# The order of loads at two places: the last quad's packs and two rows of a column product

## The chip, the cores and the metric

The kernel runs on one core of a Trainium2 chip. The metric is device time in microseconds for one execution, as the median of several runs. A core has five engines with instruction queues of their own: TensorE (PE: matmuls, with weight loads shown as PEld), VectorE (DVE), ScalarE (ACT), GpSimd (POOL) and SyncE (SP). In this kernel SyncE issues all the transfers between the memory off the core and the on-chip memory. Each engine works through its queue in the order in which it was written; semaphores order the engines among each other.

## What is computed

Four layers are applied to x of 2048 rows by 640 columns in float32. Layers 0 and 2 are attention with a sliding window, layers 1 and 3 mix x with Fourier matrices:

```python
def attention(x, wqkv, wo):            # H = 32 heads of 20, window W = 256
    q, k, v = heads(x @ wqkv)
    scores = q @ k.T * 20 ** -0.5      # for 0 <= i - j < 256, else -1e9
    return softmax(scores) @ v, heads joined, @ wo

def fourier(x):
    a, b = x @ hid_re.T, x @ hid_im.T
    return seq_re @ a - seq_im @ b

x = x + attention(layernorm(x)); x = x + fourier(layernorm(x))
x = x + attention(layernorm(x)); x = x + fourier(layernorm(x))
```

## The kernel before

Products are made with three matmuls on a high and a low part of each operand (`split`, L226 to L235: ScalarE writes the high part, VectorE or GpSimd the low part).

**An attention layer.** The 32 heads form eight quads of four heads. `heads` (L608) runs one loop of 16 steps per quad, 128 steps in all, plus a lead of ten. A step makes three things at different depths: the raw scores of row block s = step + 10 (`s_head`, L633), whose row maxima VectorE takes at L638; the transposed scores of step t = step (`t_pair`, L661, exponentials at L671, masks on GpSimd at L677 and L681); and the product with v for v = step - 1 (`pv`, L696). Every four steps the maxima are transposed, and two small transfers write them into the query tile (`m_rows`, L651).

Into each step `fill` puts a share of other matmuls (L259, in `lockstep`). First come the last projections of q and k (`project`), counted in units: 600 in all. The share is the largest of several quotients, among them "all units by step 96" (`ROWS_AT`) and "the units that the next pack needs, by the step at which it is due". Once the projection is done, `prepare(4)` (L949) posts the loads of the first four rows of x for the output parts (`load_y`, L954, tile "big", called y0, y1 and so on here), and the fill goes on with the output parts (`partials`, L956), nine matmul pairs a step. The result of a part is added to its row of x by VectorE at L980. Loads of head outputs and their factors (L861, L867) are requested along the way.

A projected piece goes to memory off the core (`qk_d`, L526) and comes back "packed" in the layout that the scores want. A pack (`pack`, L584) covers one quad and a quarter of the rows (512): twelve transfers of 80 KB at L596, the first six into the key tile and the other six into the query tile. They are deferred in triples: three at the step at which the pack is due and three at each of the next three steps. There are two key and two query tiles, for even and odd quads. The list `due` holds when each pack is due, counted in s; the last quad's four packs have entries of their own, in `LAST_DUE`. Its first raw scores are made at s = 112, that is step 102, and the second quarter's at step 106.

**A Fourier layer.** `fourier` (L1595) ends with a product by columns, in eight groups of two row blocks. Groups 1 to 5 of layer 1 (where `more` is true), and groups 1 to 7 of layer 3, take `seven` (L1711): seven products instead of eight, in the order b11, t1, b21, t2, t3, b22, t4. The right half of the odd row (`x22`) is added to after t1, the left half of the even row (`x11`) after b21. Between these additions (L1664) VectorE makes the low parts of later operands (`cut_part`, L1592), so what holds up an addition holds up the cuts behind it. Rows of x come in through `load_x` (L1649) into a ring of five tiles that other loads share, and go out through `store_x` (L1661). A row is requested by `load_x` at the head of a group's loop (L1814) or by `rows_after`, which `seven` calls behind b21. In layer 1 `rows_after` requests only one row from group 4 on, because weight chunks for the next attention layer use the ring as well.

Of the kernel before, what the change touches and what calls it, by code (L numbers as in the profile page):

```python
# [21 lines left out]
NQ = H // 4  # L22
# [8 lines left out]
AHEAD = 8  # L31
# [1 line left out]
AHEAD_X = 4  # L33
AFTER = 4
ROWS_AT = 96
LAST_DUE = (-10, -7, 2, 6)
FIRST = 7
LATE = 9
BACK = 2
# [26 lines left out]
class Net:  # L66
# [541 lines left out]
    def heads(self, xsrc, xdst, hook):  # L608
# [98 lines left out]
        def finish(quad, bk):  # L707
# [10 lines left out]
            def store():  # L718
# [6 lines left out]
        total = NCH * NSB * per_piece  # L725
        done = [2 * NSB * per_piece]

        due = [(16 * q + (4 * j - AHEAD if q < NQ - 1 else LAST_DUE[j]),
                ((-(-160 * (q + 1) // P) - 1) * NSB + 2 * (j // 2) + 2) * per_piece, q, j)
               for q in range(1, NQ) for j in range(NSB)]  # L730
        self.xsrc = xsrc
# [47 lines left out]
        for step in range(-LEAD, steps + 1):  # L779
# [11 lines left out]
            if due and s >= due[0][0]:  # L791
                while done[0] < due[0][1]:
                    fill(15)
                q, j = due.pop(0)[2:]
# [800 lines left out]
    def fourier(self, xsrc, xdst, more):  # L1595
# [53 lines left out]
        def load_x(*ts):  # L1649
            for t in ts:  # L1650
                if t < NB and t not in raws:
                    raws[t] = self.raw()
                    nc.sync.dma_start(raws[t], xsrc[t * P:(t + 1) * P, :])

        def rows_after(g):
            load_x(2 * g + 2)
            if not more or g < 4:
                load_x(2 * g + 3)

        def store_x(t):  # L1660
            nc.sync.dma_start(xdst[t * P:(t + 1) * P, :], raws.pop(t))  # L1661
# [24 lines left out]
        def eight(g, z):  # L1686
            t = 2 * g + z
            for n in range(2):
                if z:
                    coming(g + 1, n)  # L1690
                elif g:
                    self.cut_part(self.quarter(g, n, 1))
            if z == 0:
                if g:
                    self.load_u(g + 1, 1)
                    self.load_u(g + 2, 0)
                if more and g == 6:
                    before(11)
            before(t)
            ops = [self.made.popleft() for _ in range(2)]  # L1700
            for hf in range(2):
                p = self.bank("y", 320)
                cs = slice(hf * 320, (hf + 1) * 320)
                self.all3(p, [((ops[k // KC][0][k % KC], ops[k // KC][1][k % KC]),
                               (wc[k][0][:, cs], wc[k][1][:, cs])) for k in range(2 * KC)])
                add(nc.vector, raws[t][:, cs], p, raws[t][:, cs])
                if z and hf:
                    differences(g + 1)
            store_x(t)

        def seven(g, halfway):  # L1711
# [29 lines left out]
            self.cut_part(a21)  # L1741
            self.load_u(g + 1, 1)
            rows_after(g)
            halfway()
            product(y, "t2")
# [19 lines left out]
        def before(t):  # L1765
            if not more:
                return
            if t == 8:
                self.tmp = cuts(self.take_qk("kp", 0, F32), D)
                self.home = [self.home[i] for i in (2, 3, 0, 1)]  # L1770
            if 8 <= t < 11:
                for k in range(2):
                    self.prep_load(xdst, 2 * (t - 8) + k)
                if t < 10:
                    self.load_chunk(t - 8)
            i = t - 12
            if 11 <= t < NB - 1:
                for k in range(2):
                    self.prep_stats(2 * i + 2 + k)
                for k in range(2):  # L1780
                    self.prep_norm(2 * i + 2 + k)
            if t == NB - 1:
                self.prep_stats(8)
                self.prep_norm(8)

        def behind(t):
            if more and t >= 12:
                i = t - 12
                if i < 2:
                    self.cut_chunk(i)  # L1790
                for k in range(2):
                    self.prep_turn(2 * i + k)
                if i < 3:
                    for k in range(2):
                        self.prep_load(xdst, 6 + 2 * i + k)
# [15 lines left out]
        self.leave()  # L1811
        self.u_sum = [self.slot_tile(n, 512, F32)[:, :320] for n in ("rr1", "rr2", "vq2")]
        for g in range(NB // 2):
            load_x(2 * g + 1)  # L1814
            if g in sevens:
                before(2 * g)
                seven(g, lambda: before(2 * g + 1) if g < 5 else None)
            else:
                rows_after(g)
                for z in range(2):  # L1820
                    eight(g, z)
                    behind(2 * g + z)
# [73 lines left out]
```

## Time and profile before

| | |
|---|---|
| median of 3 runs | 2179.72 us (2177.11 to 2182.58) |
| the profiled execution | 2178.74 us, its span 2177.0 us |
| mean granted TensorE clock | 0.997 |
| TensorE busy | 2105.7 us, 97% |
| VectorE busy | 1625.7 us, 75% |
| ScalarE busy | 1138.3 us, 52% |
| GpSimd busy | 919.7 us, 42% |
| transfers | 414.78 MB, mean 191 GB/s |

In a row of a timeline stand the start and the duration in us, the engine (SPq is the issue of a transfer by SyncE), the line, the operation, the tiles (written <- read), the shapes and a count xN of neighbours merged into the row. In brackets stands how long the engine stood idle before it and what ended that. A row of the waits names the waiting engine and line, what it waited for, the total in us, how often, and the longest. A row of the stretches has the stretch, its length, the busy time of PE, PEld, DVE, ACT and POOL with the number of instructions, the granted clock, the busy share of the transfer engines and GB/s.

Layer 0's steps 90 to 104 lie at about 403 to 455 us, the same steps of layer 2 about 1086 us later; groups 4 and 5 of layer 1's column product lie at about 1037 to 1068 us.

### The profile page before, as it was taken

What the parts mean: (1) busy time and instruction counts of PE and PEld (TensorE: products, weight loads), DVE (VectorE), ACT (ScalarE), POOL (GpSimd) and SP (SyncE); (2) the same over time, 40 slices, a digit from 0 to 9 for tenths busy, and PEclk for the clock granted to TensorE, in tenths of its full rate; (3) what the DMA queues carried; (4) which work ended last, traced back from release to release, by engine and by line L of the source; (5) the groups of instructions that cost most, each with busy time, mean ns of one, the idle gap of its engine ahead of it and who ended that gap; (6) DMA issues with size and microseconds to landing.
All of it is one profiled execution on the core that took longest, in us unless ns stands there. A gap on an engine that the chain in (4) does not pass through costs nothing.

```text
span 2177.0 us, 48902 instructions
## 1 busy us (share of the span) xinstructions
PE 2105.7 (97%) x17812; PEld 1774.9 (82%) x17812; DVE 1625.7 (75%) x3973; ACT 1138.3 (52%) x2131; POOL 919.7 (42%) x1538
## 2 busy tenths in 40 slices
PE   7999999899999999999999999998899999999999
PEld 7987777677868888889999877776778888888899
DVE  6358888776898879786761588887868968687776
ACT  3117777656554545552341277776566645455432
POOL 3037777765513232321230377767655032331222
PEclk9999999999999999999999999999999999999999
DMA  5556666675656564757645566667855454546653
GB/s 184 176 162 191 197 189 200 204 232 165 206 188 216 177 228 160 256 186 271 209 156 172 161 191 198 189 203 202 233 157 185 141 180 135 173 135 229 240 205 136
DMA packets 234288, 414.78 MB, mean 191 GB/s; under 512 B 40768, under 2 KB 87360, under 8 KB 234048
## 3 DMA queue, kind: packets, MB, share of 16 engines
q1 hardware_dynamic: 234048, 411.66, 58.8%
q8 instruction: 141, 2.31, 0.4%
q14 instruction: 99, 0.81, 0.1%
HBM read 283.77 MB, written 126.62 MB: 189 GB/s over the span
## 4 chain that ended last, share of the span: by engine, by line
PE 81%; DVE 8%; DMA 4%; ACT 3%; issue 3%; POOL 1%; SPq 0%; ACTq 0%; DVEq 0%; POOLq 0%
PE banks L1419 29%; PE banks L259 13%; PE banks L241 13%; PE banks L1729 8%; PE banks L696 7%; PE banks L661 6%; PE banks L633 5%; DVE banks L638 1%; DVE qp L234 1%; ACT pt L671 1%; PE banks L343 1%; DMA kp<-qk_d 1%; PE banks L646 1%; DMA x_d<-x 0%; DVE big L980 0%
## 5 line engine op out<-in xcount | busy, mean ns | idle before, releaser
L638 DVE CUSTOM_DVE_ANT_0 banks<-banks,mask 128x384 f32<-128x384 f32 (+2 forms) x1024 | 527.0, 556 | 112.1 <-PE banks L633 94.7
L671 ACT ACTIVATE pt<-banks 128x768 f32<-128x768 f32 (+2 forms) x512 | 393.6, 771 | 176.4 <-PE banks L661 82.7
L677 POOL TENSOR_SCALAR_AFFINE_SELECT pt<-pt 128x256 f32<-128x256 f32 x512 | 219.0, 428 | 217.4 <-ACT pt L671 197.8
L259 PE MATMUL banks<-big,wc 64*128 64x512 f32 x1920 | 272.5, 394 | 0.4 <-DVE pt L444 0.4
L661 PE MATMUL banks<-qp,kp 61*128 61x384 f32 (+2 forms) x1024 | 209.5, 380 | 32.3 <-DVE mc L638 26.8
L696 PE MATMUL banks<-pt,vq 128*32 128x128 f32 x5760 | 210.4, 277 | 3.5 <-ACT pt L671 3.5
L633 PE MATMUL banks<-kp,qp 60*128 60x384 f32 (+2 forms) x1024 | 209.6, 351 | 1.9 <-DVE mc L638 1.8
L259 PEld LDWEIGHTS banks<-big,wc 64*128 64x128 f32 x1920 | 187.9, 185 | 21.3 <-DVE pt L444 0.5
L228 ACT ACTIVATE qp<-pt 128x512 fp32r<-128x512 f32 (+1 forms) x200 | 123.1, 625 | 135.0 <-DVE pt L1350 54.0
L681 POOL TENSOR_SCALAR_AFFINE_SELECT pt<-pt 128x256 f32<-128x256 f32 x448 | 187.6, 419 | 0.0
L661 PEld LDWEIGHTS banks<-qp,kp 61*128 61x128 f32 x1024 | 108.0, 184 | 95.6 <-DVE mc L638 73.1
L234 DVE TENSOR_TENSOR qp<-pt,qp 128x512 fp32r<-128x512 f32 (+1 forms) x198 | 155.9, 796 | 38.2 <-ACT qp L228 36.4
L696 PEld LDWEIGHTS banks<-pt,vq 128*32 128x32 f32 x5760 | 141.6, 109 | 51.6 <-issue 35.7
L1419 PE MATMUL banks<-qp,big 128*128 128x512 f32 x648 | 153.5, 390 | 0.0
L228 ACT ACTIVATE c<-pt 128x512 fp32r<-128x512 f32 x146 | 90.7, 625 | 115.8 <-POOL pt L1328 56.7
L633 PEld LDWEIGHTS banks<-kp,qp 60*128 60x128 f32 x1024 | 126.3, 186 | 25.9 <-DVE mc L638 17.0
L1348 POOL TENSOR_TENSOR pt<-pt,pt 128x512 f32<-128x512 f32 x32 | 46.8, 1461 | 237.8 <-DMA pt<-c 125.9
L638 DVE DVE_READ_ACCUMULATOR2_ANT mc<- 128x1 f32 x1024 | 143.9, 141 | 0.0
L1419 PEld LDWEIGHTS banks<-qp,big 128*128 128x128 f32 x648 | 120.7, 188 | 25.0 <-POOL qp L234 0.9
L234 DVE TENSOR_TENSOR c<-pt,c 128x512 fp32r<-128x512 f32 x144 | 116.6, 812 | 27.1 <-ACT c L228 24.3
L1419 PE MATMUL banks<-qp,xc 128*128 128x512 f32 x480 | 117.6, 391 | 3.8 <-DVE xc L234 2.3
L1419 PEld LDWEIGHTS banks<-qp,xc 128*128 128x128 f32 x480 | 89.5, 188 | 25.4 <-DVE xc L234 5.3
(241 smaller groups left out, 4401.1 us busy)
## 6 DMA issues: line engine op xcount, KB each, us to landing
pt<-c SPq DMA_DIRECT2D x166, 512.0 KB
qk_d<-c SPq DMA_DIRECT2D x80, 512.0 KB
kp<-qk_d SPq DMA_DIRECT2D x384, 80.0 KB
qp<-qk_d SPq DMA_DIRECT2D x384, 80.0 KB
kp<-u_d SPq DMA_DIRECT2D x32, 640.0 KB
o_d<-ou SPq DMA_DIRECT2D x64, 256.0 KB
x_d<-x SPq DMA_DIRECT2D x48, 320.0 KB
v_d<-pt SPq DMA_DIRECT2D x16, 768.0 KB
```

The source lines that it names most:

```text
L228: nc.scalar.activation(hi, src, AF.Copy, scale=-1.0 if neg else 1.0)
L234: (eng or nc.vector).tensor_tensor(out=lo, in0=src, in1=hi.bitcast(F32), op=OP.subtract)
L241: self.nc.tensor.matmul(p, x, y, start=n == 0, stop=n == last)
L259: self.nc.tensor.matmul(ps[a], x[r], y[r], start=half + i == 0, stop=half == 1 and i == n - 1, skip_group_check=True)
L633: nc.tensor.matmul(p, qp[quad % 2][b:b + 60, z, qb * P:(qb + 1) * P], kp[quad % 2][b:b + 60, z, k0 * P:(qb + 1) * P], start=True, stop=True)
L638: nc.vector.tensor_tensor_reduce(out=p, in0=p, in1=self.mask[:, 384 - n * P:], scale=1.0, scalar=NEG, op0=OP.add, op1=OP.max, accum_out=mc ...
L661: nc.tensor.matmul(self.banks[:, banks[e], :n * P], kp[quad % 2][b:b + 61, z, kb * P:(kb + 1) * P], qp[quad % 2][b:b + 61, z, kb * P:(kb + ...
L671: nc.scalar.activation(pt[quad, kb][:, 2 * z:2 * z + 2, :n * P], self.banks[:, b0:b1 + 1, :n * P], AF.Exp, scale=SCALE)
L677: nc.gpsimd.affine_select(out=t[:, :, 0:P], in_=t[:, :, 0:P], pattern=[[0, 2], [1, P]], compare_op=OP.is_ge, fill=0.0, base=0, channel_mul ...
L681: nc.gpsimd.affine_select(out=t[:, :, 256:384], in_=t[:, :, 256:384], pattern=[[0, 2], [-1, P]], compare_op=OP.is_gt, fill=0.0, base=0, ch ...
L696: nc.tensor.matmul(self.banks[32 * h:32 * h + 32, bank, :P], vq[:, 96 * (kb % 4) + 21 * h:96 * (kb % 4) + 21 * h + 32], t[:, h, (qb - kb) ...
L1419: nc.tensor.matmul(self.banks[:, bk, :], p, b[q], start=start and m == 0, stop=stop and last and m == 2, skip_group_check=True)
```

## The change

Two things are changed. In both attention layers the last quad's four packs are due at s = 106, 110, 114 and 118 instead of 102, 105, 114 and 118: the first at step 96 instead of 92, the second at step 100 instead of 95, the third and fourth as before. The number of units that each needs stays the same. In layer 1's column product `rows_after` of group 4 requests row 11 instead of row 10, and the head of group 5 requests row 10, where it requested row 11 before. All other rows are requested in the same order as before, in layer 3 as well.

```diff
@@ -33,7 +33,6 @@
 ROWS_AT = 96
-LAST_DUE = (-10, -7, 2, 6)
 FIRST = 7
@@ -725,7 +724,7 @@
-        due = [(16 * q + (4 * j - AHEAD if q < NQ - 1 else LAST_DUE[j]),
+        due = [(16 * q + 4 * j - AHEAD + 2 * (q == NQ - 1),
                 ((-(-160 * (q + 1) // P) - 1) * NSB + 2 * (j // 2) + 2) * per_piece, q, j)
                for q in range(1, NQ) for j in range(NSB)]
@@ -1653,9 +1652,10 @@
         def rows_after(g):
-            load_x(2 * g + 2)
             if not more or g < 4:
-                load_x(2 * g + 3)
+                load_x(2 * g + 2, 2 * g + 3)
+            else:
+                load_x(2 * g + (3 if g == 4 else 2))
@@ -1811,7 +1811,7 @@
         for g in range(NB // 2):
-            load_x(2 * g + 1)
+            load_x(2 * g, 2 * g + 1)
             if g in sevens:
```

## The prediction, made before the changed kernel was run

> **What bounds the kernel now.** I read the page first (busy shares, the chain that ended last), then the waits and the timelines of steps 90 to 104 of the two attention layers and of groups 4 and 5 of layer 1's column product, where the diff acts.
>
> ```profile
> span 2177.0 us, 48902 instructions
> ...
> PE 2105.7 (97%) x17812; PEld 1774.9 (82%) x17812; DVE 1625.7 (75%) x3973; ACT 1138.3 (52%) x2131; POOL 919.7 (42%) x1538
> ...
> PE 81%; DVE 8%; DMA 4%; ACT 3%; issue 3%; POOL 1%; SPq 0%; ACTq 0%; DVEq 0%; POOLq 0%
> ```
>
> TensorE is busy for 97% of the span and carries 81% of the chain, so moved transfers matter only where TensorE stands still. It does so twice at the same place. The waits of 427 to 437 us (layer 0, step 98) and the timelines of VectorE and TensorE around it:
>
> ```profile
> DVE big L980 <- DMA big<-x: 5.9, 1, 5.9
> PE banks L661 <- DVE mc L638: 5.8, 1, 5.8
> ```
> ```profile
> 433.09 0.82 DVE L980 TENSOR_TENSOR big<-banks,big 128x640 f32<-128x640 f32 x1 [5.91 <-DMA big<-x]
> ...
> 434.50 0.69 PE L661 MATMUL banks<-qp,kp 61*128 61x384 f32 x2 [5.79 <-DVE mc L638]
> 435.30 2.60 PE L259 MATMUL banks<-big,big 64*128 64x320 f32 x18
> ...
> 439.82 1.49 PE L259 MATMUL banks<-big,big 64*128 64x320 f32 x18
> 443.22 1.49 PE L259 MATMUL banks<-big,big 64*128 64x320 f32 x18
> ```
>
> L980 is the first addition of an output part to its row of x (tile y0). It waits 5.91 us for that row's load. The score reductions (L638) of later heads stand behind it on VectorE, so TensorE idles 5.79 us. The next 18 part matmuls take 2.60 us, against 1.49 for the same 18 one and two steps later; one step lasts 443.22 - 439.82 = 3.40 us. Layer 2 shows the same thing:
>
> ```profile
> 1519.53 0.82 DVE L980 TENSOR_TENSOR big<-banks,big 128x640 f32<-128x640 f32 x1 [5.54 <-DMA big<-x_d]
> ...
> 1520.94 0.69 PE L661 MATMUL banks<-qp,kp 61*128 61x384 f32 x2 [5.43 <-DVE mc L638]
> 1521.74 2.58 PE L259 MATMUL banks<-big,big 64*128 64x320 f32 x18
> ```
>
> The table of stretches shows the granted clock (the 1st number behind the busy times) below 1 right there:
>
> ```profile
> 426.00:436.00 10.00, 4.21 (x51) 3.56 (x51) 3.47 (x10) 2.72 (x5) 3.10 (x7) 0.79 0.86 229
> 436.00:440.00 4.00, 4.00 (x52) 3.35 (x50) 1.98 (x9) 1.20 (x4) 1.53 (x4) 0.66 0.96 286
> ```
>
> The loss, 10 x 0.21 + 4 x 0.34 = 3.5 us of full clock, spans the idle time and the slow 18 matmuls.
>
> **Why y0 is late.** SyncE's issues in layer 0 (x3 is one deferred triple of a pack):
>
> ```profile
> 413.60 1.17 SPq L596 DMA_DIRECT2D kp<-qk_d  x3
> ...
> 417.50 1.09 SPq L596 DMA_DIRECT2D kp<-qk_d  x3
> ...
> 421.95 1.12 SPq L596 DMA_DIRECT2D qp<-qk_d  x3
> 423.17 1.08 SPq L651 DMA_DIRECT2D qp<-mt  x2
> 424.29 1.21 SPq L596 DMA_DIRECT2D qp<-qk_d  x3
> 425.54 2.23 SPq L596 DMA_DIRECT2D kp<-qk_d  x6
> ...
> 428.32 1.02 SPq L954 DMA_DIRECT2D big<-x  x2
> 429.45 1.58 SPq L596 DMA_DIRECT2D qp<-qk_d  x3
> ...
> 437.44 1.81 SPq L596 DMA_DIRECT2D qp<-qk_d  x3
> ...
> 442.08 1.40 SPq L651 DMA_DIRECT2D qp<-mt  x2
> ```
> ```profile
> 417.08 0.86 PE L259 MATMUL banks<-big,wc 64*128 64x512 f32 x6
> ...
> 425.36 0.45 PE L661 MATMUL banks<-qp,kp 61*128 61x384 f32 x2 [0.66 <-DMA qp<-mt]
> ```
>
> The triples at 413.60, 417.50, 421.95 and 424.29 are the last quad's first pack (due at step 92); the six at 425.54 and the triples at 429.45 and 437.44 are its second (step 95). Two of the six and all of the first pack stand ahead of y0 and y1 (428.32), which the program posts at step 96. Their tile is free once the last projection matmul ends (417.08 + 0.86 = 417.94), so y0 is 10.4 us behind that. Also late are the maxima rows at 423.17, for which TensorE waits 0.66 us.
>
> **Edit 1: the last quad's packs, in both attention layers.** (a) The pace. A step's share of projection is the largest of several quotients. "600 units by step 96" exceeds "570 by step 92" while the pace is under (600 - 570) / (96 - 92) = 7.5 units a step; the row at 417.08 shows six matmuls, or 3 units. After the edit the first term is "570 by 96", smaller still. So no compute instruction moves: 0 us. (b) The order on SyncE. 24 transfers a layer move: triples at steps 92 to 95 go to 96 to 99, those at 95 to 98 to 100 to 103. They pass finished rows, maxima, output loads and stores, and above all the y loads; no other queue carries DMAs here. Ahead of y0 stood 12 + 6 pack transfers, now stand 3: 15 fewer. At the cheapest spacing (2.23 / 6 = 0.37 us) y0 comes 5.6 us sooner, at 422.7; at the mean of that stretch (413.60 to 428.32, 28 transfers, 0.53 us each) 7.9 us sooner, at 420.4. Landing took 433.09 - 428.32 = 4.8 us, so y0 is there at 425.2 to 427.5. L980 wants it at 433.09 - 5.91 = 427.18. The wait falls to 0 or 0.3 us; I take 0, because fewer transfers are then in flight. Layer 2:
>
> ```profile
> 1512.35 2.24 SPq L596 DMA_DIRECT2D kp<-qk_d  x6
> ...
> 1515.13 0.84 SPq L954 DMA_DIRECT2D big<-x_d  x2
> ```
>
> 5.6 us off 1515.13, plus a landing of 1519.53 - 1515.13 = 4.4, is 1513.9; wanted at 1519.53 - 5.54 = 1514.0: 0 again.
>
> (c) The gain on TensorE: 5.79 + 5.43 = 11.2 us idle. The slow 18 matmuls, (2.60 - 1.49) + (2.58 - 1.49) = 2.2 us, go too if the low clock comes from that idle time. The maxima rows at 423.17 come sooner too: 0 to 0.66 us, and I take 0.66, in layer 0 alone.
>
> On the clock the Trainium skill, page "TensorE: Matmul & The Clock Gate" (Part 1: The HAM clock gate), says that about 3.4 us of idle TensorE halve its clock and about 3.4 us of work restore it. The rows agree as far as they go: a dip behind 5.4 and 5.8 us of idleness. By the rule the 2.2 us go with the stall, as I have summed them; without it the sum would be 2.2 us smaller.
>
> (d) The cost: what is late next. The first quad-7 score matmul is that at 447.07, step 102, whose step already begins with a wait for maxima rows:
>
> ```profile
> 446.68 0.45 PE L661 MATMUL banks<-qp,kp 61*128 61x384 f32 x2 [0.82 <-DMA qp<-mt]
> 447.07 0.42 PE L633 MATMUL banks<-kp,qp 60*128 60x128 f32 x2
> ```
>
> Without stall, slow clock and this wait it would run at 447.07 - 0.82 - 5.8 - 1.1 = 439.4. It needs the first pack's last triple (step 99). Behind y0 the program has the same 22 transfers as before, through the maxima pair at 442.08 (triples of the first pack in the places of the second's); they took 442.08 + 1.40 - 428.32 = 15.2 us. From 420.4 to 422.7 that ends at 435.6 to 437.9; the triple adds 1.1 to 1.8 (its rows above) and lands 3.2 to 4.6 us behind (446.68 less the maxima pair's 443.48 or 442.08). It is there between 439.9 and 444.3, so 0.5 to 4.9 us late; net of the 0.82 us wait that it replaces, that is -0.3 to 4.1 us, and -0.8 if nothing is late. The move uses up all of its cover. I take 1 us per layer, near the early end, since fewer transfers are in flight when y0 starts; both ends stay in the range. The second pack is due three steps ahead of step 106, as the third and fourth always were, and costs 0.
>
> **Edit 2: rows 10 and 11 in layer 1.** Group 4's additions, and group 5 where it stalls:
>
> ```profile
> 1041.59 0.48 DVE L1664 TENSOR_TENSOR x<-banks,x 128x320 f32<-128x320 f32 x1
> 1043.36 0.49 DVE L1664 TENSOR_TENSOR x<-banks,x 128x320 f32<-128x320 f32 x1 [0.55 <-PE banks L1729]
> ...
> 1045.08 0.47 SPq L1653 DMA_DIRECT2D x<-x_d  x1
> ...
> 1056.32 0.32 SPq L1653 DMA_DIRECT2D x<-x_d  x1
> ...
> 1059.49 0.49 DVE L1664 TENSOR_TENSOR x<-banks,x 128x320 f32<-128x320 f32 x1 [2.42 <-DMA x<-x_d]
> ...
> 1060.77 1.73 PE L1729 MATMUL banks<-big,pt 128*128 128x320 f32 x10 [1.76 <-DVE pt L1592]
> ```
>
> Row 11, requested at 1056.32, holds VectorE 2.42 us and, through the cut behind it, TensorE 1.76 us. After the edit row 11 is the one requested at 1045.08, and row 10 lands at 1059.49. Row 10's first addition comes 1.77 us after row 11's (1043.36 - 1041.59), at 1059.49 - 2.42 + 1.77 = 1058.84, so it waits 0.65 us. That delays a cut which TensorE wants one product later, so it is covered; uncovered it costs 0.65. Bounds: gain 1.1 to 1.76 us; I take 1.76. Later rows keep their order, and layer 3 (not "more") requests as before.
>
> **Sum.** -11.2 - 2.2 - 0.7 - 1.8 + 2 x 1 = -13.9 us, against the profiled execution's 2178.74 (2177.0 span and 1.7 around it): 2164.8. The median of the runs is 2179.72, 1 us higher, so I say 2165. The runs shown spread by 5.5 us; 0.3% (6.5 us) is what a measurement can tell from no change.
>
> **Rivals.** *Half is given back*: the first pack's last triple is 3 to 5 us late at step 102 in both layers. For it: the queue behind y0 moved 22 transfers in 15.2 us, and a 4 KB maxima pair took over 3.2 us. Against: the queue starts thinner. Time: 2162.8 (the sum without the 2 us) + 2 x 4 = 2171. *All is given back*: y0 stays late, or the pack is 6 us late and the clock dips again: 2162.8 + 2 x (6 + 1.1) = 2177, within 0.3%. That is also the case in which the edit does not do what it says. *Slower*: the moved triples wait behind the large y and output loads until step 102 stands for more than 10 us. Break-even is (15.9 - 2.2) / 2 = 6.9 us a layer with the dip; at 11 us the time is 2162.8 + 2 x (11 + 1.1) = 2187. It needs the triple at 450, 6 us past my latest landing.
>
> [...]
>
> **Chances.** Forecast 0.70, half given back 0.14, all given back 0.06, slower 0.10. Faster 0.84, same 0.06, slower 0.10. Range 2160 (no wait at step 102 and the runs' spread) to 2174 (the half-back case and the spread); it leaves out the last two cases.
>
> **What would show it.** Right: L980's first wait under 1 us in both layers; no stretch under clock 1 in mid-run; first y load issued near 421; group 5's 2.42 us wait under 1. Wrong: a wait for kp or qp from qk_d at the first 60x128 score matmul above 3 us, or the L980 wait still there behind a later y0.

## The result, and the profile after

| | before | after |
|---|---|---|
| median of 15 runs each, in turn | 2181.64 us (2177.11 to 2185.82) | 2173.31 us (2167.85 to 2182.63) |
| ratio | | 0.9963, interval 0.9950 to 0.9975 |
| the profiled execution | 2178.74 us | 2174.95 us |
| mean granted TensorE clock | 0.997 | 0.995 |

The change saves 8.3 us by the medians, or 0.37% by the ratio. The prediction was 2165 us, 13.9 us below the profiled execution of before and 16.6 us below the median of before in this comparison: the direction is right, and about half of the saving came. The page after, whose lines are the busy times and the shares of the chain that ended last:

```profile
span 2173.2 us, 48906 instructions
...
PE 2110.8 (97%) x17812; PEld 1777.5 (82%) x17812; DVE 1628.4 (75%) x3973; ACT 1138.0 (52%) x2131; POOL 922.3 (42%) x1538
...
PE 80%; DVE 7%; ACT 4%; DMA 3%; issue 3%; POOL 2%; SPq 1%; ACTq 0%; DVEq 0%; POOLq 0%
```

Averages say little here: DMA's share of the chain falls from 4% to 3%, and TensorE's busy time rises by 5 us at a mean clock that is lower by 0.002. Up to about L1650 the lines of the changed kernel carry numbers that are one lower (L980 is L979, L633 is L632).

**The y0 stall is gone.** VectorE's timeline of the changed kernel at the first addition to a row of x, in layer 0:

```profile
427.68 0.82 DVE L979 TENSOR_TENSOR big<-banks,big 128x640 f32<-128x640 f32 x1 [0.51 <-PE banks L660]
```

It waits half a microsecond for TensorE, and not for the load. SyncE's issues show why, and what is late instead:

```profile
419.04 1.18 SPq L595 DMA_DIRECT2D kp<-qk_d  x3
...
420.77 1.92 SPq L953 DMA_DIRECT2D big<-x  x2
422.75 1.11 SPq L595 DMA_DIRECT2D kp<-qk_d  x3
...
429.16 2.06 SPq L595 DMA_DIRECT2D qp<-qk_d  x3
...
434.81 1.51 SPq L650 DMA_DIRECT2D qp<-mt  x2
436.36 1.20 SPq L595 DMA_DIRECT2D qp<-qk_d  x3
```

y0 and y1 are requested at 420.77, 7.6 us sooner than before. The first pack of the last quad now goes out in triples at 419.04, 422.75, 429.16 and 436.36. The last of them is the one that step 102 needs.

**A new wait has taken a part of its place.** TensorE's timeline in layer 0, and below it in layer 2:

```profile
438.82 0.22 PE L632 MATMUL banks<-kp,qp 60*128 60x128 f32 x1
441.31 0.33 PE L632 MATMUL banks<-kp,qp 60*128 60x128 f32 x1 [2.26 <-DMA qp<-qk_d]
441.31 2.52 PE L258 MATMUL banks<-big,big 64*128 64x320 f32 x18
```
```profile
1522.70 0.44 PE L660 MATMUL banks<-qp,kp 61*128 61x384 f32 x2 [2.46 <-DMA qp<-mt]
...
1524.79 0.47 PE L632 MATMUL banks<-kp,qp 60*128 60x128 f32 x1 [1.46 <-DMA qp<-qk_d]
1524.80 2.98 PE L258 MATMUL banks<-big,big 64*128 64x320 f32 x18
```

At the first matmul of the last quad TensorE stands for 2.26 us until the pack's last triple lands. In layer 2 it stands for 2.46 us for maxima rows and then for 1.46 us for the pack. Behind each wait the 18 part matmuls run slowly, in 2.52 and 2.98 us; at full clock they take 1.49. The stretches (PE, PEld, DVE, ACT and POOL busy, then the granted clock) put a size to that:

```profile
442.00:446.00 4.00, 4.00 (x47) 3.31 (x46) 1.36 (x6) 1.01 (x3) 0.87 (x3) 0.59 0.83 223
...
1524.00:1531.00 7.00, 6.21 (x58) 5.32 (x60) 1.88 (x8) 1.85 (x6) 2.92 (x6) 0.52 0.93 243
```

Lost clock is 4 x 0.41 = 1.6 us in layer 0, and 7 x 0.48 = 3.4 us in layer 2, of which 0.4 us fell into time in which TensorE waited anyway.

**The balance.** The transposes of the maxima come every four steps (L646, L645 after). Stretches between the same ones can be set side by side: first those of before, then those of after.

```profile
427.90:449.00 21.10, 14.18 (x194) 11.85 (x193) 10.55 (x38) 8.14 (x14) 8.72 (x21) 0.84 0.94 287
449.00:463.30 14.30, 12.59 (x205) 10.65 (x202) 11.92 (x40) 8.75 (x16) 10.38 (x21) 1.00 0.76 197
463.30:476.40 13.10, 12.70 (x202) 10.53 (x202) 10.93 (x38) 7.93 (x15) 8.39 (x19) 1.00 0.78 214
...
1514.70:1535.40 20.70, 13.61 (x194) 11.63 (x193) 10.55 (x38) 8.14 (x14) 8.50 (x20) 0.84 0.93 257
1535.40:1549.70 14.30, 12.59 (x205) 10.65 (x202) 11.92 (x40) 8.75 (x16) 10.56 (x22) 1.00 0.87 251
```
```profile
427.90:444.20 16.30, 13.41 (x195) 11.20 (x194) 10.68 (x38) 8.10 (x15) 9.65 (x22) 0.93 0.92 273
444.20:459.00 14.80, 13.09 (x202) 10.96 (x201) 11.66 (x40) 8.70 (x16) 9.75 (x20) 0.96 0.73 187
459.00:473.30 14.30, 12.96 (x203) 10.60 (x202) 11.13 (x38) 8.02 (x15) 8.56 (x19) 1.00 0.72 196
...
1509.50:1528.10 18.60, 14.04 (x194) 11.70 (x193) 10.66 (x38) 8.23 (x14) 9.58 (x21) 0.89 0.91 251
1528.10:1543.20 15.10, 13.69 (x203) 11.21 (x202) 11.37 (x40) 8.75 (x16) 9.69 (x20) 0.91 0.82 208
```

The first stretch of each layer holds the stall and its removal: 4.8 us shorter in layer 0, 2.1 us in layer 2. The following ones give 0.5 + 1.2 us back in layer 0 and 0.8 us in layer 2. The 1.2 us is the third pack, whose last triple is now late too. The waits of 460 to 475 us in the changed kernel:

```profile
PE banks L632 <- DMA qp<-qk_d: 0.9, 1, 0.9
```

With the stretches on both sides, where little differs, layer 0 takes 68.6 us (404.7 to 473.3) where it took 72.0 (404.4 to 476.4), and layer 2 84.4 us (1486.2 to 1570.5, rounded) where it took 86.3 (1490.7 to 1577.0): 3.4 + 1.9 = 5.3 us saved. Edit 2 adds 1.8 to that, 7.1 in all. The pair of profiled runs differs by only 3.8 us: the one after lost clock at three other places, which can have cost it up to 5.1 us (see the last section). The medians differ by 8.3.

**Edit 2.** VectorE in group 5 of the changed kernel: row 11's addition waits for nothing, and row 10's waits 1.11 us for its load. TensorE has no gap there any more.

```profile
1054.57 0.48 DVE L1664 TENSOR_TENSOR x<-banks,x 128x320 f32<-128x320 f32 x1
...
1056.89 0.49 DVE L1664 TENSOR_TENSOR x<-banks,x 128x320 f32<-128x320 f32 x1 [1.11 <-DMA x<-x_d]
```

### The profile page after: what moved, and what is told of

Its sections match the earlier page's. It is cut to its first block, busy times and chain, and to the rows that moved or that the text cites. A ratio compares the mean times of both kernels' runs of the same rounds, so it can differ in the third digit from the quotient of the medians.

```text
span 2173.2 us, 48906 instructions
## 1 busy us (share of the span) xinstructions
PE 2110.8 (97%) x17812; PEld 1777.5 (82%) x17812; DVE 1628.4 (75%) x3973; ACT 1138.0 (52%) x2131; POOL 922.3 (42%) x1538
## 4 chain that ended last, share of the span: by engine, by line
PE 80%; DVE 7%; ACT 4%; DMA 3%; issue 3%; POOL 2%; SPq 1%; ACTq 0%; DVEq 0%; POOLq 0%
PE banks L1418 29%; PE banks L258 13%; PE banks L240 12%; PE banks L1729 8%; PE banks L695 7%; PE banks L660 6%; PE banks L632 5%; DVE banks L637 1%; ACT pt L670 1%; DMA qp<-qk_d 1%; DVE qp L233 1%; DMA kp<-qk_d 1%; PE banks L342 1%; ACT big L1040 1%; POOL rs L1088 1%
## 5 line engine op out<-in xcount | busy, mean ns | idle before, releaser
L660 PE MATMUL banks<-qp,kp 61*128 61x384 f32 (+2 forms) x1024 | 210.1, 381 | 21.4 <-DVE mc L637 16.3
L632 PE MATMUL banks<-kp,qp 60*128 60x384 f32 (+2 forms) x1024 | 210.1, 350 | 6.1 <-DMA qp<-qk_d 4.7
L632 PEld LDWEIGHTS banks<-kp,qp 60*128 60x128 f32 x1024 | 126.3, 186 | 30.6 <-DVE mc L637 16.2
L233 DVE TENSOR_TENSOR c<-pt,c 128x512 fp32r<-128x512 f32 x144 | 111.7, 777 | 27.3 <-ACT c L227 24.8
```

Source lines behind the costliest of these rows:

```text
L233: (eng or nc.vector).tensor_tensor(out=lo, in0=src, in1=hi.bitcast(F32), op=OP.subtract)
L632: nc.tensor.matmul(p, qp[quad % 2][b:b + 60, z, qb * P:(qb + 1) * P], kp[quad % 2][b:b + 60, z, k0 * P:(qb + 1) * P], start=True, stop=True)
L660: nc.tensor.matmul(self.banks[:, banks[e], :n * P], kp[quad % 2][b:b + 61, z, kb * P:(kb + 1) * P], qp[quad % 2][b:b + 61, z, kb * P:(kb + ...
```

## The experiments

The theory after the result: y0 was late because pack transfers stood ahead of it on SyncE, and moving the first pack by four steps made that pack itself late, with a stretch of half clock behind each wait. The rivals: edit 2 brought most of the gain; or the transfer engines are simply full at these steps, so that any order loses about the same. Diffs are against the kernel before, unless they say "after". "Edit 2" stands for the last two hunks of the change.

| run | last quad's packs at steps | edit 2 | ratio to before | interval | us |
|---|---|---|---|---|---|
| after | 96, 100, 104, 108 | yes | 0.9963 | 0.9950 to 0.9975 | -8.1 |
| e1_packs_only | 96, 100, 104, 108 | no | 0.9982 | 0.9971 to 0.9994 | -3.9 |
| e2_rows_only | 92, 95, 104, 108 | yes | 0.9993 | 0.9983 to 1.0002 | -1.5 |
| e3_second_only | 92, 100, 104, 108 | no | 0.9961 | 0.9948 to 0.9975 | -8.5 |
| e4_first_at_94 | 94, 100, 104, 108 | yes | 0.9940 | 0.9927 to 0.9953 | -13.1 |
| e8_six_a_step | as after, first in 2 steps | yes | 0.9967 | 0.9954 to 0.9980 | -7.2 |
| e5_two_ahead | as after, 2 y ahead | yes | 0.9942 | 0.9926 to 0.9959 | -12.6 |
| e7_six_ahead | as after, 6 y ahead | yes | 0.9995 | 0.9983 to 1.0006 | -1.1 |
| e6_y_on_act | as before | no | 1.0071 | 1.0057 to 1.0085 | +15.5 |
| e9_94_two_ahead | as e4, 2 y ahead | yes | 0.9933 | 0.9916 to 0.9949 | -14.6 |
| e10_step_sooner | 94, 99, 103, 107, 2 y ahead | yes | 0.9935 | 0.9918 to 0.9951 | -14.2 |

The last column is the ratio less 1, times the time of before in the same comparison (2179.5 to 2182.8 us). For after that gives 8.1 us, where the medians differ by 8.3.

**The two edits apart: e1 and e2.** e1 has edit 1 alone:

```diff
-LAST_DUE = (-10, -7, 2, 6)
+LAST_DUE = (-6, -2, 2, 6)
```

> Edit 1 alone. Theory (two races on the transfer queue: the wait for y0 is gone in both layers, the wait for the last triple of the first pack at step 102 has come in its place and gives back part): about 6.5 us faster than before (3 to 10), with the step-102 wait of 1.5 to 4 us in both layers. Rival (the gain of the whole change comes from the rows, edit 2): within 2 us of before.

Measured: 3.9 us faster. Its waits of 436 to 446 us show the pack and the maxima at step 102:

```profile
PE banks L633 <- DMA qp<-qk_d: 1.8, 1, 1.8
...
PE banks L661 <- DMA qp<-mt: 1.1, 1, 1.1
```

e2 has edit 2 alone:

```diff
-            load_x(2 * g + 2)
             if not more or g < 4:
-                load_x(2 * g + 3)
+                load_x(2 * g + 2, 2 * g + 3)
+            else:
+                load_x(2 * g + (3 if g == 4 else 2))
...
-            load_x(2 * g + 1)
+            load_x(2 * g, 2 * g + 1)
```

> Edit 2 alone. Theory: 1.8 us faster (0 to 3), too little to be told from no change; in the profile TensorE's 1.76 us of idle time in group 5 is gone, and the wait for y0 stays at 5 to 6 us in both layers. Rival (the gain comes from the rows): 6 to 9 us faster.

Measured: 1.5 us faster, not told from nothing. The gap in group 5 is gone from the trace, and the y0 wait is where it was (waits of 425 to 445 us):

```profile
DVE big L980 <- DMA big<-x: 5.6, 1, 5.6
```

So edit 2 doesn't carry the gain. The product of the two ratios is 0.9975, at the end of the interval of the whole change; whether the edits help each other beyond their sum stays open.

**Which pack holds y0 up: e3.** The first pack stays where it was, the second moves.

```diff
-LAST_DUE = (-10, -7, 2, 6)
+LAST_DUE = (-10, -2, 2, 6)
```

> The kernel before, with the last quad's second pack alone moved (step 100 instead of 95); the first stays at step 92, the rows stay as before. 12 instead of 18 pack transfers then stand ahead of y0. Theory (each transfer ahead of y0 costs its place in the queue, 0.37 to 0.53 us): y0 comes 2.2 to 3.2 us sooner, its wait falls from 5.9 and 5.5 us to 2.3 to 3.7 us in each layer, and step 102 waits for no pack; 5 to 9 us faster than before. Rival (y0 is late for the bytes in flight from the projection's end, whatever the packs): wait above 5 us, within 2 us of before.

Measured: 8.5 us faster, without edit 2. The second pack alone is worth more than both (e1). Its y loads go out at 425.81, 2.3 us sooner than before when both are counted from the same step; a part of the wait remains, the larger one in layer 2 (its issues in layer 0, its waits in layer 2):

```profile
425.81 1.31 SPq L954 DMA_DIRECT2D big<-x  x3
```
```profile
DVE big L980 <- DMA big<-x_d: 3.6, 1, 3.6
```

TensorE does not wait for a pack at step 102; it waits 2.3 us for the third pack at step 110 of layer 0. So the second pack was free to move, and the first was not.

**The first pack moved by two steps: e4.** With edit 2:

```diff
-LAST_DUE = (-10, -7, 2, 6)
+LAST_DUE = (-8, -2, 2, 6)
```

> The changed kernel, but with the first pack of the last quad due at step 94 instead of 96, the second at 100 as changed. Theory (order on the queue decides): y0 comes about 2.5 us later than in the changed kernel and is waited for 0 to 1 us; the last triple stands ahead of most of the large loads, so the step-102 wait for it is gone: 13 to 16 us faster than before. Rival (the bytes moved between 418 and 450 us bound the stretch, in whatever order): 5 to 10 us faster, as the changed kernel.

Measured: 13.1 us faster. This profiled run is some 3 us ahead of that of the changed kernel when it comes to these steps (its maxima are transposed in step 98 at 424.73, against 427.90), so times are compared from a step, here from the first exponential of step 95. From there y0 is requested after 6.6 us in layer 0 and 6.1 in layer 2, where it was 3.3 and 4.6 in the changed kernel and 11.2 and 11.6 before: nine pack transfers stand ahead of it instead of three or 18. The pack's last triple goes out at 421.79, long ahead of step 102:

```profile
420.90 0.84 SPq L954 DMA_DIRECT2D big<-x  x2
421.79 1.11 SPq L596 DMA_DIRECT2D qp<-qk_d  x3
...
433.69 1.18 SPq L651 DMA_DIRECT2D qp<-mt  x2
```

No half clock is left in steps 98 to 103, and of the waits at step 102 only those for maxima, 1.5 us in layer 0 and 0.7 in layer 2. This settles the main question: the part of the gain that was missing lay in the place of the first pack. Against the number of pack transfers ahead of y0, TensorE's idle time for it in layers 0 and 2 is 5.8 and 5.4 us with 18 (before), 1.5 and 3.5 with 12 (e3), 0.8 and 1.2 with 9 (e4), and none with 3 (after).

**The first pack at the same step, in two steps instead of four: e8.** Against after:

```diff
-                    defer(i // 3, f)
+                    defer(i // (6 if (q, j) == (NQ - 1, 0) else 3), f)
```

> The changed kernel, but the first pack of the last quad is issued six transfers a step (steps 96 and 97) instead of three (96 to 99). Theory (order decides): y0 comes 1.2 us later, still in time within 0.7 us; the last triple comes two steps sooner in the queue and is not waited for at step 102; what may be left there is the wait for the maxima rows, up to 2.5 us: 11 to 15 us faster than before. Rival (bytes bound the stretch): 5 to 10 us faster.

Measured: 7.2 us faster than before, where more than after had been expected: a miss. The pack is in time (its second half leaves at 424.03), but now the maxima rows are last. They are requested at 437.33, 2.0 us later than in the changed kernel when both are counted from the same step, and TensorE waits 3.1 us for them in layer 0 and 2.5 us in layer 2:

```profile
424.03 3.23 SPq L595 DMA_DIRECT2D qp<-qk_d  x6
...
437.33 1.23 SPq L650 DMA_DIRECT2D qp<-mt  x2
```
```profile
PE banks L660 <- DMA qp<-mt: 3.1, 1, 3.1
```

One wait took the place of the other. What is scarce at these steps is room, not one transfer's place: the transfer engines are busy for 0.91 to 0.94 of the stretch of 16 to 21 us in both kernels (the balance above, the share before the GB/s). The next two runs change the load itself.

**Less and more load in front of step 102: e5 and e7.** Both against after. e5 requests two y loads ahead instead of four, e7 six (with one a step instead of one every other step):

```diff
-AHEAD_X = 4
+AHEAD_X = 2
```
```diff
-AHEAD_X = 4
+AHEAD_X = 6
...
-                self.post(2 * t, lambda t=t: self.load_y([t]))
+                self.post(t, lambda t=t: self.load_y([t]))
```

> The changed kernel with the rows of x for the output parts requested two parts ahead instead of four, so that two large loads (y3 and y4) come behind the maxima pair and the last triple in the queue instead of ahead of them; packs as changed. Theory (large loads ahead of the small transfers set the step-102 wait): the wait falls by 1 to 2 us in each layer, and the half-clock stretches behind it get fewer: 11 to 15 us faster than before. Rival (it is the lateness of the packs themselves, whatever large loads lie between): 6 to 10 us faster, as the changed kernel, with the waits of 2.3 and 3.9 us kept.

> The changed kernel with six rows of x posted at once, one slot apart, and six parts ahead: two more large loads ahead of the maxima pair and the last triple. Theory: about 2 us more wait at step 102 in each layer: 0 to 6 us faster than before. Rival (lateness of the packs alone): 6 to 10 us faster.

Measured: e5 is 12.6 us faster than before, e7 1.1 us, so the gain is gone. In e7 TensorE waits at step 102 for both (waits of 430 to 450 us). In layer 2 these waits are 4.1 and 1.5 us, and each layer has 6.8 us of half clock there:

```profile
PE banks L660 <- DMA qp<-mt: 3.1, 1, 3.1
...
PE banks L632 <- DMA qp<-qk_d: 1.7, 1, 1.7
```

In e5 the wait at step 102 of layer 0 is under 0.5 us, but the third pack's last triple is now 3.1 us late, at step 110 (waits of 460 to 480 us):

```profile
PE banks L632 <- DMA qp<-qk_d: 3.1, 1, 3.1
```

In layer 2 the expected fall did not come: e5 still waits 1.7 us for maxima and 1.8 us for the pack at step 102, where the changed kernel waited 2.5 and 1.5. Two loads of 320 KB less, or more, in front of step 102 move the time from after's -8.1 us to -12.6, or to -1.1. So the y loads ahead bear on the step-102 wait in layer 0, and in both layers of e7; why layer 2 kept its wait in e5 stays open.

**y0 past the queue: e6.** ScalarE's queue requests y0 and y1, and the packs stay as before:

```diff
-                self.nc.sync.dma_start(...)
+                eng = self.nc.scalar if t < 2 else self.nc.sync
+                eng.dma_start(...)
```

> The kernel before, with packs and rows as they were, but the loads of y0 and y1 issued by ScalarE instead of SyncE. Theory (the place behind the packs in SyncE's queue made y0 late): y0 is requested near 421 us, its wait falls from 5.9 and 5.5 us to under 2 us, and there is no wait for the packs at step 102: 8 to 14 us faster than before. Rival (the bytes in flight made y0 late, not its place): the y0 wait stays above 4 us: within 4 us of before.

Measured: 15.5 us slower, a clear miss. ScalarE's issue of y0, then SyncE's own timeline around it, SyncE's waits, and VectorE:

```profile
421.36 0.40 ACTq L955 DMA_DIRECT2D big<-x  x1
```
```profile
418.45 0.35 SPq L623 DMA_DIRECT2D vq<-v_d  x1
425.06 1.78 SPq L596 DMA_DIRECT2D qp<-qk_d  x3
```
```profile
SPq L596 <- DMA big<-x: 7.1, 2, 6.2
```
```profile
430.84 0.25 DVE L716 RECIPROCAL rc<-sm 128x16 f32<-128x16 f32 x1 [6.66 <-DMA sm<-ou]
```

y0 came in time. But SyncE stood from 418.80 to 425.06 in front of a pack transfer until y0 had landed, a load that ScalarE requested only at 421.36. All that SyncE had still to request came 6 us later, and VectorE waited 6.66 us for the softmax sums. The reason is on record in the trace: each transfer's record names the semaphore that it counts up as its parts land. All 1972 transfers use eight semaphores (100 to 105, 107 and 109) in turn, in the order of the program, whichever engine issues them, and none is issued before the transfer that had its semaphore last has landed. y0 has semaphore 101, and its place in that order lies between SyncE's issues of 413.47 and 415.46. Its parts land from 423.79 to 425.04; the next transfer with 101 is the one that SyncE issues at 425.06. y1 has 103: its last part lands at 426.55, and SyncE issues the next one at 426.57. y0's own wait is gone, as the theory says, but the time doesn't tell the theories apart, since the run brought in a stall of its own.

**Both remedies together: e9 and e10.** e9 is e4 with two y loads ahead; e10 has all packs but the first one step sooner as well, against the wait at step 110:

```diff
-AHEAD_X = 4
+AHEAD_X = 2
-LAST_DUE = (-10, -7, 2, 6)
+LAST_DUE = (-8, -3, 1, 5)
```

(e9: `LAST_DUE = (-8, -2, 2, 6)`.)

> The changed kernel with the first pack due at step 94 and the rows of x two parts ahead. Theory: what was left of the step-102 wait in the run with step 94 (1.5 us for the maxima rows in layer 0) goes as well: 14 to 17 us faster than before, 0 to 3 faster than with step 94 alone. Rival: no different from step 94 alone, 13 us faster than before.

> The last quad's packs due at steps 94, 99, 103 and 107, the rows of x two parts ahead, the rows of the column product as changed. Theory (the waits at step 110, 0.6 to 3.1 us where the queue had no stall ahead of it, are the third pack's last triple, three steps ahead and too late): those waits go, the second pack stays clear of step 106: 14 to 18 us faster than before, 0 to 3 faster than with 94, 100, 104, 108. Rival (a step sooner only crowds the maxima rows and loads of steps 99 to 103): 8 to 13 us faster.

Measured: 14.6 and 14.2 us faster than before, not told apart from each other. In e9 the waits at step 102 are gone and a y0 wait of 2.2 us is back in layer 0 (waits of 420 to 450 us). The same nine pack transfers stand ahead of y0 as in e4, where it was 0.8 us, so their number alone doesn't set the wait:

```profile
DVE big L980 <- DMA big<-x: 2.2, 1, 2.2
```

In e10 neither is left in layer 0, nor the wait at step 110; in layer 2 a y0 wait of 1.7 us is. Its stretches between the same transposes as above:

```profile
428.30:441.10 12.80, 12.19 (x194) 10.23 (x193) 10.28 (x38) 8.06 (x14) 8.68 (x21) 1.00 0.99 287
...
1503.90:1518.20 14.30, 12.30 (x195) 10.26 (x194) 10.61 (x38) 8.12 (x14) 8.81 (x21) 1.00 1.00 272
```

12.8 us in layer 0 (21.1 before, 16.3 after) and 14.3 in layer 2 (20.7 and 18.6), at full clock, with transfer engines that are busy for 0.99 and 1.00 of the time. So full transfer engines alone don't set the time: in layer 0 the same four steps run without a stall. They do so on fewer bytes, about 3.7 MB (GB/s times length) against 6.1 before and 4.4 after; the rest goes later, where the engines have room (0.72 busy in the next four steps). e4, e9 and e10 are all faster than both kernels, against after by about 5 to 6.5 us (their ratios to before, less after's, times 2180; the intervals of e4 and after just touch).

## Why the prediction was right, and where it was wrong

**Right.** (a) The pace: the part matmuls come in the same groups at the same steps, and the extra time is in waits. (b) The order: y0 was to be requested between 420.4 and 422.7; it was at 420.77. Its wait is gone in both layers, as taken. (c) The gain: from the starts of the exponentials, steps 97 to 99 take 7.54 us less than before in layer 0 and 7.12 us less in layer 2; together 14.7, against 11.2 + 2.2 + 0.7 = 14.1 in the sum. Edit 2: the 1.76 us gap is gone; row 10's wait is 1.11 us instead of 0.65, and covered as said. Of the four signs of being right, L980's wait and y0's issue came; the clock did not stay at 1 in mid-run, and the wait in group 5 stayed just above 1 us.

**Wrong: step (d), "I take 1 us per layer, near the early end, since fewer transfers are in flight when y0 starts".** By the same starts, steps 102 and 110 of layer 0 cost 3.49 + 1.11 us more than before, less 0.61 at step 101, where the old wait for maxima has gone; steps 101 and 102 of layer 2 cost 1.11 + 3.98 more. That is 9.1 us where the sum had 2, more than the whole shortfall. The term has three parts.

First, the waits. Layer 0's was 2.26 us, and it replaced 0.82: 1.4 net, well inside the stated -0.3 to 4.1 and near the 1 us taken. Demand came at 438.82 + 0.22 = 439.04 (439.4 had been worked out) and the triple at 441.31 (439.9 to 444.3). Layer 2 was carried over from layer 0 without a look at its own queue. There the waits were 2.46 + 1.46 = 3.9 us and replaced 1.3, as the waits of before at 1524 to 1536 us show:

```profile
PE banks L661 <- DMA qp<-mt: 1.3, 1, 1.3
```

That is 2.6 net, and the two layers together 4.0 instead of 2. The reason given for the early end fell: the queue isn't thinner. The transfers that leave the space ahead of y0 return behind it, into a stretch in which the transfer engines are busy for 0.92 of the time.

Second, half clock. That the slow 18 matmuls "go too" was true of step 98, but the sum had no price for half clock behind the new, shorter wait. It costs 1.6 us in layer 0 and 3.0 us in layer 2: 4.6 us, the largest part. That takes back all the clock that was gained: before, 4.2 and 3.2 us of half clock met work (from the end of each gap, at 434.50 and 1520.94, to the end of the half clock at 438.72 and 1524.16), a loss of 3.7 us, of which the sum had counted the 2.2 us that fell on 18 matmuls. The Trainium skill, page "TensorE: Matmul & The Clock Gate" (Part 1, HAM oscillation), says as its rule that TensorE should have no idle gaps over about 3.4 us. By that rule the waits of layer 0 cost no clock; the trace doesn't agree, with 3.4 us of half clock behind a gap of 2.26 us, and the measurement decides.

Third, the later packs. "The second pack is due three steps ahead of step 106, as the third and fourth always were, and costs 0" was argued from due steps alone. SyncE's queue was shifted, and the third pack's last triple came 0.9 us late.

4.0 + 4.6 + 0.9 = 9.5 us is close to the 9.1 measured by steps. That 2173.3 still lies in the range of 2160 to 2174 is owed to the range's upper end, which was set by a rival, and not to this sum. Of the rivals, *half is given back* (2171 us) named the right place and about the right size; it had wrongly taken the pack as the only late transfer, where in layer 2 the maxima rows were the first. The sign "a wait for kp or qp from qk_d at the first 60x128 score matmul above 3 us" was not reached by 2.26 us; it stood too high, since the wait carries the clock loss with it.

## What to carry to other kernels

When a transfer is moved out of the way of another in a stretch whose transfer engines are full, look for what will then be the last to land, and price that wait in each place by the place's own rows, with the half clock that may follow it. Move by the least that frees the late load; here two steps instead of four kept the gain without a wait for the pack. A request put on another engine's queue is not free of the first queue: here both share eight semaphores.

## What the runs showed of the hardware

**At most eight transfers are under way at a time.** The trace's records show it by the semaphores told at e6: of the 1972 transfers of the kernel before, none is issued until the one eight places ahead of it has landed. The key-tile transfer issued at 425.54 lands at 428.99, and SyncE issues the second y load, eight places on, at 429.00; the next three pairs are 429.43 and 429.45, 429.78 and 429.80, 430.73 and 430.75. So once eight are under way, a place in SyncE's queue costs the landing of what stands ahead, and not only the time of issuing it.

**Half clock comes in steps of 3.41 us on a fixed grid.** In the twelve profiles 46 stretches of half clock lie in mid-run. Each lasts 3.41 us or a multiple (6.83, once 10.24), and within one profile all begin on one grid of 3.41 us: in the changed kernel at 441.88, 639.85, 1523.90, 1605.82 and 1677.50, which are 58, 259, 24 and 21 times 3.413 us apart. Each of the 46 begins behind a grid window in which TensorE was busy for less than 0.65. Three such windows of the changed kernel:

```profile
438.47:441.88 3.41, 1.15 (x19) 0.92 (x13) 1.08 (x5) 1.59 (x4) 2.92 (x6) 1.00 0.95 248
636.44:639.85 3.41, 1.88 (x8) 1.00 (x7) 3.38 (x7) 2.40 (x5) 0.00 (x0) 1.00 0.73 228
1520.49:1523.90 3.41, 0.62 (x3) 0.40 (x3) 0.49 (x4) 1.28 (x3) 1.25 (x3) 1.00 0.91 242
```

And two windows of the grid of before that no half clock followed; the second holds the same gap of 1.4 us as that at 636.44 above:

```profile
565.01:568.42 3.41, 1.66 (x8) 1.12 (x7) 3.41 (x7) 2.29 (x5) 1.90 (x3) 1.00 0.46 175
```
```profile
640.10:643.52 3.42, 2.02 (x8) 1.39 (x9) 3.39 (x6) 2.05 (x4) 0.00 (x0) 1.00 0.75 230
```

A share of 1.88 / 3.41 = 0.55 was followed by half clock, and one of 2.02 / 3.42 = 0.59 was not. But the share alone doesn't decide it. At the same place of e8 a share of 1.91 / 3.41 = 0.56 was not followed either, nor was 1.66 / 3.41 = 0.49 at 565.01 above:

```profile
638.32:641.73 3.41, 1.91 (x7) 1.30 (x8) 3.38 (x7) 2.08 (x4) 0.00 (x0) 1.00 0.76 231
```

Of the grid windows at full clock in the twelve profiles (without the first 25 us and the end), all 18 with a share under 0.47 were followed by half clock, and of those between 0.47 and 0.65 only 28 of 100. So a gap of 1 to 2 us may cost its own length or 1.7 us more, and what decides it stays open. The same page of the Trainium skill, in Part 1, gives a free-running window of 3413 ns, and the grid agrees with that.

**A stall may hide the clock loss that it causes.** Before, the half clock of layer 0 began at 431.89, inside the 5.8 us gap, and 2.6 of its 6.8 us fell into it. After, the gap of 2.26 us ended just ahead of the window's end, and all 3.41 us met work.

**The runs' times go with the clock.** Among the 15 runs after, those at a mean clock of 0.997 to 0.998 took 2167.9 to 2173.4 us and the two at 0.993 took 2180.9 and 2182.6; 0.001 of the mean clock is 2.2 us of full clock over the span. The profiled run after (0.995) had three stretches of half clock, at 639.85, 1605.82 and 1677.50, that the profiled run before had not: 3 x 1.7 = 5.1 us. With them its lead of 3.8 us would be up to 8.9, and the medians gave 8.3.
